# Reordering scatters, gathers and transposes in a chunk-select attention and top-1 expert kernel

## The chip, the cores and the metric

The kernel runs on one core of a Trainium2 chip. The metric is the device time of one launch in microseconds, the median of several runs. The core has four compute engines that run their own instruction streams and meet at semaphores: TensorE (PE in the profile, its weight loads PEld), VectorE (DVE), ScalarE (ACT) and GpSimd (POOL). SyncE (SP) only issues transfers. In this kernel SyncE issues the loads of q, k and v and all transposes done by DMA; GpSimd issues the weight loads and every indirect transfer (scatter and gather of token rows, scatter of the output).

## The reference

The computation has two halves. The first is attention for 4 batches, 8 heads, 768 positions and 64 elements per head, in which each query attends to six chunks of 32 keys, chosen by an upper bound made from each chunk's smallest and largest key:

```python
ub = np.sum(np.maximum(q[:, :, :, None, :] * k_min[:, :, None, :, :],
                       q[:, :, :, None, :] * k_max[:, :, None, :, :]), axis=-1)
ub = np.where(causal, ub, -1000000000.0)
top_chunks = np.argsort(ub, axis=-1)[..., -top_k:]
scores = scale * np.matmul(q, k.transpose(0, 1, 3, 2))
# mask = chunk selected and causal; softmax over what is left
return np.matmul(attn, v)
```

The second half takes the 3072 tokens of 512 elements that come out and sends each through one of 8 experts:

```python
logits = x @ w_gate
expert_idx = np.argmax(logits, axis=1)
# gate_w: the softmax probability of the chosen expert
for e in range(E):
    xe = x[expert_idx == e]
    out[expert_idx == e] = gate_w[...] * (np.maximum(xe @ w1[e], 0.0) @ w2[e])
```

## The kernel before

Two heads of a batch are one pair; there are 16 pairs, four to a batch, and one pass of the main loop for each. In pass `i` the kernel computes scores and outputs of pair `i`, prepares keys and queries of pairs `i+1` and `i+2`, and works off the router's part of pair `i-1`. The order on TensorE and GpSimd is the order in which the code is written (`manual_schedule`); in the pass loop that holds for VectorE too. ScalarE and SyncE are ordered by the scheduler, SyncE by hand in the expert part.

The steps of preparing a query (`pn` is pair `i+1`, `pj` pair `i+2`):

```python
def q_t(hf):                                   # TensorE: transpose half a query into PSUM
    pt = ps_m.tile([128, 384], FP32, tag="m")  # ps_m: 3 buffers, shared by all small results
    ...
def q_v(hf): nc.vector.tensor_copy(out=qT[:], in_=s[f"qp{hf}"][:])
def q_r(hf): nc.gpsimd.tensor_scalar(qA[:], s[f"qT{hf}"][:], 0.0, None, ALU.max)
def q_c(hf): nc.gpsimd.tensor_copy(out=qsb[0:64, 0, ts(hf, 384)], in_=s[f"qT{hf}"][0:64, :])   # cast
def q_s(hf): nc.scalar.activation(qsb[0:64, 1, ts(hf, 384)], s[f"qp{hf}"][64:128, :], AF.Copy)
def mask():                                    # TensorE: transpose the selection, 6 matmuls (L379)
    pt = ps_m.tile([64, S], BF16, tag="m")
    ...
```

Scores, outputs and denominators. `Pr` and `Pa` hold exponentials, `po` the output of one query half in PSUM (one buffer), and `ud` multiplies the summed exponentials with a column of ones, and the output with the router's weights:

```python
def scores(i, u):   # matmuls into ps (L407), Exp on ScalarE (L412), causal select on GpSimd (L416)
def av(i, u):       # po += v x P (L429)
def out_t(i, qb):   # VectorE: ot <- po (L435), frees po
def add(i, u):      # VectorE: Pa += P (L441), 128 x 768 float32
def ud():           # TensorE: pu <- Pa, ot, Pr (L464), needs all adds of the pair
```

The main loop of before, cut to what the change touches:

```python
av(i - 1, 6); out_t(i - 1, 1); load(i + 1, "v")
scores(i, 0); scores(i, 1)
r["ud"]()
if pn: pn["q_v"](1); pn["q_r"](1)
...
    route[b - 1]["rank_v"](); route[b - 1]["gate"]()       # third pair of a batch
weights(4 * i); scatters(i, 0); early(i, 0)
if i == NP - 2: table(True)
keys(j, lambda: scores(i, 2))                              # key transposes of pair i+2
av(i, 0); scores(i, 3); av(i, 1); add(i, 1); out_t(i, 0)
if pn: pn["ub"]()
...
if pn: pn["q_c"](0); pn["q_c"](1)
weights(4 * i + 1); scatters(i, 1); early(i, 1)
r["lgp_t"](); r["x_t"](0)
if pn: pn["select_t"]()
r["lgp"](); r["xr"](0)
if pn: pn["select"]()
scores(i, 4); av(i, 2)
weights(4 * i + 2); scatters(i, 2)
scores(i, 5); av(i, 3); scores(i, 6)
early(i, 2)
r["x_t"](1)
if pj: pj["q_t"](0); pj["q_t"](1); load(i + 3, "q")
r["xr"](1)
early(i, 3)
if pn: pn["mask"]()
av(i, 4)
if pj: pj["q_v"](0); pj["q_r"](0); pj["q_s"](0); pj["q_s"](1)
add(i, 3); add(i, 4); add(i, 5)
av(i, 5)
if hp == 1 and b > 0: route[b - 1]["rank"]()               # 12 small matmuls (L553 to L559)
weights(4 * i + 3); scatters(i, 3); early(i, 4)
```

Routing. When the four pairs of a batch are done, `logits`, `gate`, `rank` and `rank_v` give every token a row in `xs_dram`, sorted by expert, and `scatter(us)` writes the rows of one batch there, in six scatters of 128 tokens. `table(first)` is about 20 small VectorE instructions that work out which expert and which rows each tile of 128 tokens has. It runs twice: `table(True)` for the first NA = 11 tiles, which hold tokens of the first three batches only, and `table(False)` for the others, when the last batch is ranked.

A tile of the expert part:

```python
def gather(j):      # GpSimd: 128 rows of xs_dram -> xg_bufs[j % XB]   (XB = 8)
def x_in(j):        # SyncE: transpose by DMA, xT <- xg; then, from j = 4, tok(j)
def tok(j):         # VectorE: token numbers of the tile (L702, L704), for the output scatter
def up(j):          # TensorE: ph <- w1, xT (L715, 8 matmuls); ScalarE: h_ = relu; SyncE: hT <- h_ (L721)
def down(j):        # TensorE: py <- w2, hT (L731, 8 matmuls); ScalarE: y = gate * py (L737);
                    # GpSimd: scatter y into out (L738)
```

```python
dve.__exit__(None, None, None)            # from here on the scheduler orders VectorE
av(NP - 1, 6); out_t(NP - 1, 1)
late = list(range(6))
for n in range(4): tok(n)
with tc.manual_schedule(engines={SP, POOL}):
    up(0); rt["ud"](); up(1); x_in(4); rt["lgp_t"](); rt["x_t"](0); rt["x_t"](1); rt["lgp"]()
    r["logits"](); r["gate"](); rt["xr"](0); rt["xr"](1)
    up(2); x_in(5); down(0)
    r["rank"](); r["rank_v"](); table(False)
    # then for each tile j from 3:
        if j + 5 < hi:
            if late: r["scatter"](late[:2]); del late[:2]
            gather(j + 5)
        if j < hi: up(j)
        if j + 3 < hi: x_in(j + 3)
        if j - 2 >= lo: down(j - 2)
```

The gathers 0 to 7 are issued in the last pass of the pair loop, by `early`. 28 tiles are computed; three more are computed only if a count in the table asks for it.

## Time and profile before

The median of three runs is 362.26 us (361.37 to 362.64). The profiled execution took 368.39 us, its span from the first to the last instruction is 366.6 us.

| part of the span | from, us | to, us |
|---|---|---|
| start, pair 0 | 0 | 29.0 |
| passes 0 to 14, from one mask transpose to the next | 29.0 | 232.2 |
| last pass, up to the first expert tile | 232.2 | 247.4 |
| expert tiles 0 to 27 and the end | 247.4 | 366.6 |

How to read what follows: busy time is the union of an engine's instructions; a table of stretches gives it for any window. The timeline lists instructions in order of time, with the idle time of their engine ahead of them in square brackets and the instruction or transfer that ended it. L and a number is the line of the kernel. A wait for several semaphores is put down to the one that came last by the profile.

### The profile page before, as it was taken

How to read it: one execution, taken by the hardware profiler on the slowest of the kernel's cores; microseconds unless marked ns; L12 is line 12 of the kernel's file. 1: busy time of each engine (PE TensorE's matmuls, PEld its weight loads, DVE VectorE, ACT ScalarE, POOL GpSimd, SP SyncE). 2: the span in 40 equal slices, each digit the busy share in tenths (PEclk: the TensorE clock that was granted, in tenths of full speed). 3: DMA queues.
4: the chain of work that ended last, by engine and by line, in shares of the span. 5: the costliest groups of instructions: out<-in, count | busy, mean ns of one | idle time of the engine just before them, and what ended most of it. 6: DMA issues, size and time to landing. Idle time of an engine off the chain costs nothing.

```text
span 366.6 us, 8002 instructions
## 1 busy us (share of the span) xinstructions
PE 336.7 (92%) x2599; PEld 188.4 (51%) x2599; DVE 223.4 (61%) x748; ACT 225.6 (62%) x369; POOL 223.8 (61%) x333
## 2 busy tenths in 40 slices
PE   7779999999999999999999997979969799999980
PEld 3345666666656656565566663544423344444430
DVE  8778988979999889989788999645600000000000
ACT  3578777887787677778777864642342355445530
POOL 7437656566369994359985737774556655555331
PEclk9999999999999999999999999899999999999996
DMA  9988997999269999837999932146969999999850
GB/s 180 182 166 153 231 228 159 189 228 187 46 136 168 220 217 185 144 88 153 206 198 155 188 56 83 45 102 118 176 161 203 222 199 206 214 188 212 168 142 28
DMA packets 138184, 59.85 MB, mean 163 GB/s; under 512 B 122779, under 2 KB 130973, under 8 KB 138144
## 3 DMA queue, kind: packets, MB, share of 16 engines
q1 hardware_dynamic: 120608, 29.91, 42.0%
q0 software_dynamic: 17536, 29.42, 41.1%
q8 instruction: 23, 0.38, 0.4%
q14 instruction: 17, 0.14, 0.1%
HBM read 56.14 MB, written 10.51 MB: 182 GB/s over the span
## 4 chain that ended last, share of the span: by engine, by line
PE 46%; issue 16%; DVE 13%; POOL 13%; ACT 4%; DMA 2%; SPq 2%; POOLq 1%; DVEq 0%; ACTq 0%
PE po L429 14%; PE ps L407 8%; PE pu L464 6%; DVE Pa L441 4%; PE pu L350 4%; POOL out_dram L738 4%; PE ph L715 3%; PE pt L226 3%; PE xp L505 2%; PE py L731 2%; PE pt L244 2%; POOL xs_dram L579 2%; POOL KTE L680 2%; POOL xg L680 1%; DMA QSB<-spare 1%
## 5 line engine op out<-in xcount | busy, mean ns | idle before, releaser
L412 ACT ACTIVATE Pr<-ps 128x768 f32<-128x768 f32 (+2 forms) x112 | 66.8, 627 | 28.0 <-PE ps L407 26.1
L441 DVE TENSOR_TENSOR Pa<-Pa,Pr 128x768 f32<-128x768 f32 (+2 forms) x80 | 68.0, 850 | 7.6 <-PE po L429 2.3
L429 PE MATMUL po<-Pr,v 128*64 128x384 f32 (+2 forms) x448 | 63.8, 401 | 2.1 <-POOL Pr L416 2.1
L731 PE MATMUL py<-w_all,hT 128*128 x224 | 52.9, 379 | 3.4 <-DMA hT<-h__4156 1.3
L407 PE MATMUL ps<-QSB,KTE 128*64 128x384 bf16 (+2 forms) x576 | 55.0, 295 | 0.3 <-ACT QSB L326 0.2
L416 POOL TENSOR_SCALAR_AFFINE_SELECT Pr<-Pr 128x256 f32<-128x256 f32 x80 | 36.1, 475 | 21.8 <-ACT Pr L412 21.0
L407 PEld LDWEIGHTS <-KTE 128*64 128x64 bf16 x576 | 31.4, 110 | 26.9 <-issue 22.5
L429 PEld LDWEIGHTS po<-Pr,v 128*64 128x64 f32 x448 | 33.8, 137 | 17.8 <-POOL Pr L416 5.9
L253 POOL TENSOR_SCALAR qA<-qT 128x384 f32<-128x384 f32 x28 | 41.3, 1476 | 2.0 <-DVE qT L249 1.3
L731 PEld LDWEIGHTS <-hT 128*128 128x128 bf16 x224 | 21.9, 98 | 30.4 <-DMA hT<-h__4156 1.7
L238 ACT ACTIVATE KTE<-pt 64x384 bf16<-64x384 f32 x64 | 30.9, 482 | 4.8 <-PE pt L226 3.2
L412 ACT ACTIVATE Pa<-ps 128x768 f32<-128x768 f32 x32 | 25.9, 811 | 8.4 <-PE ps L407 7.0
L715 PE MATMUL ph<-w_all,KTE 128*128 x120 | 28.4, 379 | 2.5 <-ACT h__4156 L719 1.5
L429 PE MATMUL po<-Pa,v 128*64 128x384 f32 x128 | 26.8, 499 | 2.3 <-DVE ot L435 2.3
L738 POOL DMA_INDIRECT out_dram<-y,ti x14 | 13.9, 990 | 21.7 <-ACT y L737 19.9
L715 PE MATMUL ph<-w_all,QSB 128*128 x104 | 24.6, 379 | 1.5 <-issue 1.4
L579 POOL DMA_INDIRECT xs_dram<-xrow,sli x21 | 22.1, 1054 | 6.0 <-issue 5.5
L195 POOL DMA_DIRECT2D w_all<-in_moe_w_dram x32 | 25.3, 790 | 0.0
L234 DVE TENSOR_REDUCE kmx<-pt 128x12 f32<-128x384 f32 x32 | 17.8, 556 | 12.1 <-PE pt L226 8.5
L464 PE MATMUL pu<-Pa,dcol 128*32 128x384 f32 x128 | 20.6, 498 | 0.3 <-DVE Pa L441 0.2
L256 POOL CAST QSB<-qT 64x384 bf16<-64x384 f32 x32 | 17.2, 563 | 6.0 <-DVE qT L249 3.0
L715 PEld LDWEIGHTS <-KTE 128*128 128x128 bf16 x120 | 11.6, 97 | 17.4 <-issue 4.8
(210 smaller groups left out, 584.6 us busy)
## 6 DMA issues: line engine op xcount, KB each, us to landing
w_all<-in_moe_w_dram POOLq DMA_DIRECT2D x32, 512.0 KB
q<-in_q_dram SPq DMA_DIRECT2D x32, 192.0 KB
v<-in_v_dram SPq DMA_DIRECT2D x32, 192.0 KB
k<-in_k_dram SPq DMA_DIRECT2D x16, 192.0 KB
w_all<-in_k_dram SPq DMA_DIRECT2D x16, 192.0 KB
xs_dram<-xrow,sli POOLq DMA_INDIRECT x21
out_dram<-y,ti POOLq DMA_INDIRECT x14
xg<-xs_dram,grow POOLq DMA_INDIRECT x12
```

The costliest lines, as they stand in the source:

```text
L238: nc.scalar.activation(kte[0:64, hd, ts(hf, 384)], s[f"kp{hf}"][64 * hd:64 * hd + 64, :], AF.Copy, bias=0.0, scale=0.125)
L253: nc.gpsimd.tensor_scalar(qA[:], s[f"qT{hf}"][:], 0.0, None, ALU.max)
L407: nc.tensor.matmul(pv[c:c + CW, hd, :], lhsT=kte[:, hd, ds(kb * 128 + c, CW)], rhs=qsb[:, hd, ds(qb * 384 + 384 - w, w)], start=True, stop ...
L412: nc.scalar.activation(P[:, :, ds(c0, w)], pv, AF.Exp)
L416: nc.gpsimd.affine_select(out=pd, in_=pd, pattern=[[0, 2], [1, 128]], compare_op=ALU.is_ge, fill=0.0, base=0, channel_multiplier=-1)
L429: nc.tensor.matmul(s["po"][64 * hd:64 * hd + 64, 384 - w:384], lhsT=vt[:, kb, hd, :], rhs=P[:, hd, ds(c0, w)], start=first, stop=last and ...
L441: nc.vector.tensor_tensor(acc[:, :, 384 - w:384], acc[:, :, 384 - w:384], P[:, :, ds(c0, w)], ALU.add)
L464: nc.tensor.matmul(pu[32 * g:32 * g + 32, 384 - w:384], lhsT=lhsT, rhs=rhs, skip_group_check=True, **kw)
L579: d = nc.gpsimd.indirect_dma_start(out=xs_dram[:], out_offset=bass.IndirectOffsetOnAxis(ap=sli[:, u:u + 1], axis=0), in_=bst[b][f"xrow{u % ...
L715: nc.tensor.matmul(ph[:, fh, :], lhsT=xT[:, c, :], rhs=w_all[:, ds(wo + (c * F + fh * 512), 512)], start=(c == 0), stop=(c == NDC - 1), sk ...
L731: nc.tensor.matmul(py[:], lhsT=hT[:, c, :], rhs=w_all[:, ds(wo + (W1W + c * DM), DM)], start=(c == 0), stop=(c == NFC - 1))
L738: d = nc.gpsimd.indirect_dma_start(out=out[:], out_offset=bass.IndirectOffsetOnAxis(ap=ti[:], axis=0), in_=y, in_offset=None, bounds_check ...
```

## The change

The change moves instructions and adds buffers (three for gathered tiles, one for queries); the arithmetic stays. It is for taking GpSimd's casts, scatters and gathers and VectorE's table out of the way of steps that TensorE waits for, and for spreading the transfers of the expert part. Its parts:

- the second half of the query transposes and its copies go behind the mask transposes; the ud matmuls go behind the key transposes; one add goes ahead of the mask
- the casts of the query on GpSimd go ahead of scatters and weight issues of the pass, and one scatter of each batch moves behind the last score group of its pass
- the first table goes behind the chunk selection
- odd pairs' queries are loaded into a part of the weight buffer that is filled late, so that query loads have two buffers; three weight blocks instead of two are loaded at the start, and the block that shares that buffer late
- all eleven gathers of the first tiles are issued ahead of the expert tiles, into eleven buffers, in other places of the last pass
- the last batch's scatters go out one per tile, from tile 3 on, the first ahead of it, instead of two
- later gathers start at tile 8, and their transposes are issued two tiles ahead instead of three
- VectorE keeps its written order in the expert part too, with the token copies in fixed places

```diff
-    EARLY = 2
+    EARLY = 3
...
-        if nm == "k" and i % 2:
-            at = (E - 1) * WE + W1W + 4 * DM
+        if nm in "kq" and i % 2:
+            at = (E - 1) * WE + (W1W + 4 * DM if nm == "k" else 2 * F)
...
-    XB = 8
+    XB = NA
     def gather(j):
-        if 4 <= j < 8:
+        if 8 <= j < NA:
+            if j == 8:
+                more_x = work.tile([128, 3, XW], BF16, tag="xrow00", name="more_x")
+                xg_bufs.extend(more_x[:, n] for n in range(3))
+        elif 4 <= j < 8:
...
     def early(i, slot):
         if i == NP - 1:
-            for n in ((0, 1), (2, 3), (4, 5), (6, 7), ())[slot]:
+            for n in ((0, 1), (), (2, 3, 4), (5, 6, 7), ())[slot]:
                 gather(n)
...
             scores(i, 1)
-            r["ud"]()
+            if hp == 2 and b > 0:
+                route[b - 1]["rank_v"]()
             if pn:
                 pn["q_v"](1)
+                pn["q_s"](1)
                 pn["q_r"](1)
+                pn["q_c"](0)
+                pn["q_c"](1)
...
             weights(4 * i)
             scatters(i, 0)
             early(i, 0)
-            if i == NP - 2:
-                table(True)
-            keys(j, lambda: scores(i, 2))
+
+            def mid():
+                r["ud"]()
+                scores(i, 2)
+
+            keys(j, mid)
...
             if pn:
                 pn["select"]()
+            if i == NP - 2:
+                table(True)
...
             r["x_t"](1)
             if pj:
                 pj["q_t"](0)
-                pj["q_t"](1)
-                load(i + 3, "q")
             r["xr"](1)
+            add(i, 3)
             early(i, 3)
             if pn:
                 pn["mask"]()
+            if pj:
+                pj["q_t"](1)
+                load(i + 4, "q")
             av(i, 4)
...
         with tc.manual_schedule(engines={SP, POOL}):
+            for n in range(8, NA):
+                gather(n)
             up(0)
...
             rt["x_t"](1)
+            tok(0)
+            tok(1)
             rt["lgp"]()
...
             r["rank_v"]()
+            r["scatter"]((0,))
+            tok(4)
+            tok(5)
             table(False)
...
-                    if lo == 0 and j + 5 < hi:
-                        if late:
-                            r["scatter"](late[:2])
-                            del late[:2]
-                        gather(j + 5)
+                    if lo == 0 and j < 8:
+                        r["scatter"]((j - 2,))
+                    if lo == 0 and 8 <= j < hi - 3:
+                        gather(j + 3)
                     if j < hi:
                         up(j)
-                    if lo == 0 and j + 3 < hi:
-                        x_in(j + 3)
+                    if lo == 0 and j + 3 < NA or lo == 0 and j >= NA - 2 and j + 2 < hi:
+                        n = j + (3 if j + 3 < NA else 2)
+                        x_in(n)
+                        tok(n)
                     if j - 2 >= lo:
                         down(j - 2)
             tiles(0, JM)
+        dve.__exit__(None, None, None)
```

## The prediction

> **What bounds the kernel now.** I read the page's busy totals first, then a table of stretches cut at events of the kernel, and last the timeline inside the stretches that come out long.

> ```profile
> PE 336.7 (92%) x2599; PEld 188.4 (51%) x2599; DVE 223.4 (61%) x748; ACT 225.6 (62%) x369; POOL 223.8 (61%) x333
> ```

> TensorE at 92% says that it is the bound, not what can be won. For that I cut the span at the mask transposes (L379), which come once in each pass of the pair loop, and in the expert part at the first matmul of a tile. Columns: span, busy time (and count) of each engine, granted clock, DMA share, GB/s.

> ```profile
> 72.19:86.17 13.98, 13.98 (x132) 9.05 (x132) 11.73 (x37) 11.00 (x19) 8.90 (x17) 1.00 1.10 204
> 100.14:114.81 14.67, 14.16 (x144) 8.80 (x144) 13.65 (x48) 11.07 (x19) 11.31 (x17) 1.00 0.75 137
> 128.98:143.55 14.57, 14.48 (x131) 8.50 (x131) 12.32 (x37) 11.01 (x19) 10.06 (x18) 1.00 1.16 218
> 171.98:187.13 15.15, 13.88 (x131) 8.18 (x131) 12.63 (x37) 11.49 (x20) 13.93 (x20) 1.00 1.02 195
> 215.21:232.22 17.01, 14.25 (x131) 7.84 (x130) 14.59 (x58) 8.58 (x14) 10.72 (x16) 0.90 0.19 56
> 265.07:293.01 27.94, 22.34 (x97) 9.32 (x96) 1.28 (x9) 9.60 (x12) 17.36 (x18) 1.00 0.90 198
> 293.01:349.00 55.99, 55.68 (x257) 25.01 (x256) 2.30 (x14) 28.28 (x33) 28.28 (x28) 1.00 0.95 200
> ```

> The reader is to see a floor and what stands above it. Six of the thirteen stretches between mask transposes last 13.97 or 13.98 us with TensorE busy throughout: there it is packed, and no reordering can shorten them. The other seven are 14.67, 14.17, 14.57, 14.45, 15.15, 14.10 and 17.01. In the expert part a tile needs 16 matmuls of 0.216 us (1.73 us from one group's start to the next), 3.45 us; 265.07 to 293.01 holds six tiles, 27.94 instead of 20.7, and 293.01 to 349.00 holds sixteen at 3.50. So some 6 us in the pair loop and 7 us in the expert tiles are waits. The timeline names most of them (start, length, what ran, idle before it and its releaser):

> ```profile
> 172.47 2.57 POOL L416 TENSOR_SCALAR_AFFINE_SELECT Pr<-Pr 128x256 f32<-128x256 f32 x3
> 228.11 1.55 PE L429 MATMUL po<-Pa,v 128*64 128x384 f32 x4 [2.32 <-DVE ot L435]
> 245.35 1.52 PE L429 MATMUL po<-Pr,v 128*64 128x384 f32 x12 [1.34 <-POOL Pr L416]
> 270.39 1.92 PE L715 MATMUL ph<-w_all,KTE 128*128 x8 [1.47 <-ACT h__4156 L719]
> 273.60 1.89 PE L731 MATMUL py<-w_all,hT 128*128 x8 [1.29 <-DMA hT<-h__4156]
> ```

> At 172 us the causal selects on GpSimd start only after 8 us of casts, scatters and weight issues in a row (164.86 to 172.47). At 228 TensorE waits for the copy that empties po, because VectorE has just worked off the first table, 221.26 to 226.38. At 245 four gathers stood ahead of the selects (238.93 to 244.26). From 262 on it is transfers: ScalarE's wait for h__4156, 6.8 us, is the longest there, and the trace doesn't say convincingly what released it.

> [...] two selects took 1.48 us at 232.57 and a scatter 1.51 at 234.22 beside VectorE's adds, against 0.77 and 0.97 to 1.1 elsewhere. [...] from 300 to 345 us the two queues take 65.1% and 32.9%. [...] the last hT transpose shows 1.23 us from 352.02, and TensorE uses its data at 355.30.

> **The change part by part.** No arithmetic goes away: the count of matmuls, activations and transfers stays. Everything is order, and three buffers.

> *Pair loop.* (a) The denominator matmuls (ud) move behind the key transposes, the add of unit 3 ahead of the mask. In 128.98 to 143.55 the chain of waits runs through three adds of 1.10, 1.34 and 1.08 us that end at 133.10, and ud starts at 133.15; with 0.8 us of key transposes ahead of it and one add earlier, that 0.6 us is hidden. (b) The query's second transposes go behind the mask transposes, so that the mask need not find its PSUM bank as a fourth beside three others (bufs=3); the trace shows 0.7 us of waits for it in all. (c) The casts go ahead of scatters and weight issues. That takes nothing off GpSimd (13.93 of 15.15 us busy in the worst stretch), but the casts are now out of the way before the selects matter. Of the six long stretches before the last, the surplus over 13.98 is 0.69+0.19+0.59+0.47+1.17+0.12 = 3.2 us; 0.45 us in two of them is the rank matmuls, real work. Of the 2.3 us left I take three quarters: **-1.8**.

> (d) The first table moves behind the selection, when po has been emptied. The 2.32 us wait at 228 goes. But its 5 us of VectorE work now stands before three adds, 3.1 us, in a pass where VectorE works 14.59 us, so a part may come back as a wait for the accumulators: **-2.0**.

> *Entry to the expert part.* (e) Two gathers instead of four ahead of the selects, and VectorE kept in program order, so that the token copies (L702, waiting for gathers at 242.25, 243.49, 244.99, 246.33) no longer hold up the adds: TensorE can start the first tile 1.4 us earlier and its later 0.25 us wait goes, about -1.8. (f) Against it: nine gathers now come in a row on GpSimd. One takes 1.0 us and the next starts 0.30 later, so 9 x 1.32 = 11.9 us, from 244.3 to 256.2, and behind them stands the addition of the last logits (0.65 us), which ran at 255.09. From its end to the one-hot took 1.5 us: 256.9 + 1.5 = 258.4, against the rank matmuls at 257.87 now. The gain of (e) is thus lost again at the rank matmuls: **0**.

> *Tiles.* (g) Before, tiles 3 to 5 each issue two scatters, a gather and an output scatter: four at 1.3 us, 5.2 us of GpSimd in a 3.45 us tile, and the transfers on top of transposes. After, tiles 3 to 7 have one scatter and one output, 2.6 us, and gathers 8 to 10 fall into a stretch with the DMA engines some 60% busy (244 to 256). If this overload is the cause, most of the 7.2 us goes; since h__4156's wait isn't explained, I take a little over half: **-4.0**. (h) From tile 11 on the input transpose is issued two tiles ahead, not three, and it stands behind the hidden transpose on SyncE. In the steady part tile 24 starts at 338.64, its hT transpose at 341.66 (3.02 later), the input transpose behind it at 342.99 (4.35 later). The packets of both, about 1,600, counted microsecond by microsecond, end some 6.7 us after that tile's start and 6.4 us after tile 22's; with the 0.3 us or so between the last tile's hT packets (about 355.0) and their use at 355.30, data are ready at 6.7 to 7.0. Needed: 2 x 3.453 = 6.91. That is a tie. At 0.05 us a tile for 16 tiles: **+0.8**.

> (i) A third early weight and a second query buffer: the first 44 us wait for VectorE (13.61 of 15.24 us busy in 29.00 to 44.24), so nothing: **0**.

> Sum: -1.8 - 2.0 + 0 - 4.0 + 0.8 = **-7.0 us**; 362.26 - 7.0 = **355.3 us**.

> **The rivals.** *The input transpose becomes the bound* (h). With the wait for both transposes at 8 us instead of 6.9, a tile takes 4.0 us, since the loop closes over two tiles: (4.35 + 3.65)/2. Sixteen tiles cost 9 us and the time is about 362 to 364. For it: the DMA engines are 99% busy from 300 to 345. Against it: the packet counts. *The gather chain starves the tiles:* gathers from 11 on now start at tile 8, only one tile ahead of their transpose. Gather 11 starts some 2.4 us into tile 8 and lands about 3.3 us after its start (238.93 to 242.25 in the first one), 5.7; its transpose is issued at 3.45 + 4.35 = 7.8. It holds with 2 us to spare. *Nothing of the tile part is won,* because the 7.2 us come from something else than the order of GpSimd's transfers, or belong to the profiled execution only (its device time was 368.39 us against 362.26): then (g) is 0 and the time is 359. *Everything is won:* (d), (g) and (a) to (c) in full give -3 -7 -2.3 +0.8, about 351.

> **Range and chances.** The middle case is 355.3. The full gain, 351, sets the low end at 350.5; the tie in (h) turning out badly while the rest holds, 355.3 + 5, sets the high end at 360.5. Faster by 2% means under 355.0, so the middle lies on the line: 0.45. Slower by 2% needs 369.5, more than the worst rival: 0.05. Within 2%: 0.50.

> **What will show it.** (a) to (c): the six stretches near 14.0, with 14.4 where rank lies. (d): no wait of po for ot L435 in pass 14. (e), (f): the first tile starts earlier against the mask before it, and a wait of 1 to 2 us ahead of pr L553 on VectorE's one-hot. (g): tiles 5 to 11 at about 3.6 us each. (h): no waits, or short ones, of PEld L715 (its new line) for KTE and QSB transposes from tile 11 on; tiles at 3.5. The prediction is wrong if that last number is 3.7 or more, or if tiles 5 to 11 stay at 4.6.

## The result, and the profile after

The changed kernel takes 394.67 us (median of four executions, 393.15 to 395.22) against 362.45 us for the kernel before (361.37 to 362.67) on the same chip: ratio 1.0889, 95% interval 1.0851 to 1.0927. It is slower by 32 us where 7 us of gain were predicted.

First the page's engine totals of the changed kernel:

```profile
PE 337.8 (86%) x2599; PEld 182.1 (47%) x2599; DVE 221.3 (57%) x748; ACT 226.2 (58%) x369; POOL 230.0 (59%) x333
```

TensorE is busy 337.8 us against 336.7, and the span is 391.0 against 366.6 us: all but about a microsecond of the difference is time in which TensorE waits. Where it waits, the table of stretches of the changed kernel shows, cut at the same events (span, busy time and count of PE, PEld, DVE, ACT, POOL, then granted clock, DMA share, GB/s). The first line is one plain pass of the pair loop, the second pass 14, then from the last mask to tile 0, tiles 0 to 5, 5 to 11, and 11 to 27:

```profile
59.80:74.61 14.81, 13.77 (x131) 8.34 (x131) 11.55 (x37) 10.97 (x20) 9.01 (x14) 1.00 1.01 181
227.33:240.43 13.10, 13.10 (x134) 7.65 (x134) 11.55 (x42) 8.81 (x15) 10.64 (x13) 1.00 0.28 47
240.43:261.66 21.23, 15.91 (x125) 7.95 (x124) 12.85 (x32) 8.44 (x14) 13.19 (x20) 0.84 0.32 79
261.66:283.30 21.64, 18.60 (x106) 8.48 (x106) 10.67 (x57) 7.00 (x9) 13.93 (x16) 0.92 0.76 163
283.30:306.12 22.82, 20.88 (x98) 9.40 (x96) 0.99 (x8) 10.95 (x13) 12.80 (x13) 1.00 1.06 219
306.12:373.47 67.35, 57.14 (x257) 24.94 (x257) 2.38 (x15) 26.67 (x31) 29.49 (x30) 1.00 0.74 164
```

| stretch | before, us | after, us | difference |
|---|---|---|---|
| start to the last mask | 232.22 | 240.43 | +8.2 |
| last mask to tile 0 | 15.15 | 21.23 | +6.1 |
| tiles 0 to 5 | 17.70 | 21.64 | +3.9 |
| tiles 5 to 11 | 27.94 | 22.82 | -5.1 |
| tiles 11 to 27 | 55.99 | 67.35 | +11.4 |
| tile 27 to the end | 17.6 | 17.5 | -0.1 |

The sum is +24.4 us, the difference of the two spans. It is less than the 32 us between the medians because the profiled execution of the kernel before was six microseconds longer than its median, and that of the changed kernel 1.5 us shorter.

The waits stand in the timeline of TensorE in the changed kernel (start, length, what ran, and in brackets the idle time before it and what ended it):

```profile
65.40 0.85 PE L464 MATMUL pu<-Pa,dcol 128*32 128x384 f32 x8 [1.04 <-ACT QSB L266]
249.07 0.86 PE L464 MATMUL pu<-Pa,dcol 128*32 128x384 f32 x3 [4.24 <-DVE Pa L441]
274.45 0.22 PE L553 MATMUL pr<-oh,U 128*128 128x48 bf16 x1 [2.06 <-DVE oh L530]
323.60 1.89 PE L717 MATMUL ph<-w_all,QSB 128*128 x8 [2.42 <-DMA QSB<-xg]
332.44 1.89 PE L717 MATMUL ph<-w_all,QSB 128*128 x8 [1.77 <-DMA QSB<-xg]
```

There are four kinds, one for each loss. **At 65.40** the denominator matmuls (ud) wait for ScalarE's copy q_s(1) (L266). ud reads nothing that this copy writes; the two have only a PSUM pool in common. The page's group table of the changed kernel shows that this is the rule (busy, mean ns | idle before, releaser):

```profile
L464 PE MATMUL pu<-Pa,dcol 128*32 128x384 f32 x128 | 15.8, 536 | 17.7 <-ACT QSB L266 13.5
```

13.5 us of idle time stand ahead of ud for this copy alone. **At 249.07** ud waits for the additions, which stand behind the table on VectorE. VectorE's timeline, from the table's last operation on:

```profile
245.36 0.17 DVE L646 SCALAR_TENSOR_TENSOR grow<-ej,loc 128x11 int32<-128x11 f32 x1
245.44 0.55 DVE L509 TENSOR_TENSOR xrow<-xp,rec 128x384 bf16<-128x384 f32 x1
245.91 3.10 DVE L441 TENSOR_TENSOR Pa<-Pa,Pr 128x768 f32<-128x768 f32 x3
```

**At 274.45** the rank matmuls wait for the one-hot. It is made from the last logits, and their addition on GpSimd runs only at 272.52, behind nine gathers in a row (260.53 to 272.50). **From tile 11 on** the tiles wait for their input transposes.

### The profile page after: what moved, and what is told of

Same layout as the page of the kernel before. It is cut to its first block, busy times and chain, and to the rows that moved or that the text cites. A ratio compares the mean times of both kernels' runs of the same rounds, so it can differ in the third digit from the quotient of the medians.

```text
span 391.0 us, 8009 instructions
## 1 busy us (share of the span) xinstructions
PE 337.8 (86%) x2599; PEld 182.1 (47%) x2599; DVE 221.3 (57%) x748; ACT 226.2 (58%) x369; POOL 230.0 (59%) x333
## 4 chain that ended last, share of the span: by engine, by line
PE 45%; issue 18%; DVE 12%; POOL 10%; ACT 6%; DMA 6%; POOLq 1%; DVEq 0%; ACTq 0%
PE po L429 15%; PE ps L407 9%; PE pu L464 6%; PE pu L350 6%; DVE Pa L441 5%; ACT Pr L412 3%; POOL out_dram L740 3%; PE xp L505 2%; PE pt L244 2%; POOL xg L684 2%; PE lgp L483 2%; ACT QSB L266 2%; POOL xs_dram L579 2%; PE selp L358 2%; DMA more_x<-xs_dram,grow 2%
## 5 line engine op out<-in xcount | busy, mean ns | idle before, releaser
L412 ACT ACTIVATE Pr<-ps 128x768 f32<-128x768 f32 (+2 forms) x112 | 66.8, 628 | 27.0 <-PE ps L407 24.2
L441 DVE TENSOR_TENSOR Pa<-Pa,Pr 128x768 f32<-128x768 f32 (+2 forms) x80 | 65.9, 823 | 19.6 <-PE po L429 14.1
L429 PE MATMUL po<-Pr,v 128*64 128x384 f32 (+2 forms) x448 | 62.0, 399 | 0.3 <-POOL Pr L416 0.3
L416 POOL TENSOR_SCALAR_AFFINE_SELECT Pr<-Pr 128x256 f32<-128x256 f32 x80 | 43.6, 568 | 30.1 <-ACT Pr L412 29.5
L253 POOL TENSOR_SCALAR qA<-qT 128x384 f32<-128x384 f32 x28 | 38.7, 1383 | 3.8 <-DVE qT L249 3.7
L429 PEld LDWEIGHTS po<-Pr,v 128*64 128x64 f32 x448 | 30.1, 137 | 20.4 <-issue 11.7
L412 ACT ACTIVATE Pa<-ps 128x768 f32<-128x768 f32 x32 | 25.9, 808 | 14.4 <-PE ps L407 14.4
L717 PE MATMUL ph<-w_all,KTE 128*128 x120 | 28.3, 379 | 5.6 <-DMA KTE<-xg 1.7
L717 PE MATMUL ph<-w_all,QSB 128*128 x104 | 26.0, 394 | 7.4 <-DMA QSB<-xg 4.2
L464 PE MATMUL pu<-Pa,dcol 128*32 128x384 f32 x128 | 15.8, 536 | 17.7 <-ACT QSB L266 13.5
L579 POOL DMA_INDIRECT xs_dram<-xrow,sli x21 | 24.3, 1159 | 5.6 <-issue 4.7
L429 PE MATMUL po<-Pa,v 128*64 128x384 f32 x128 | 26.7, 498 | 0.0
L740 POOL DMA_INDIRECT out_dram<-y,ti x14 | 13.8, 988 | 21.1 <-ACT y L739 21.1
L195 POOL DMA_DIRECT2D w_all<-in_moe_w_dram x32 | 25.6, 801 | 0.0
L234 DVE TENSOR_REDUCE kmx<-pt 128x12 f32<-128x384 f32 x32 | 17.6, 548 | 8.4 <-ACT KTE L238 8.2
L499 POOL TENSOR_TENSOR lg<-lg,lgt 128x48 f32<-128x48 f32 x24 | 6.9, 289 | 24.4 <-DVE lgt L490 23.4
L509 DVE TENSOR_TENSOR xrow<-xp,rec 128x384 bf16<-128x384 f32 x28 | 15.4, 552 | 10.4 <-PE xp L505 10.3
```

Of the source, the lines that this page charges most:

```text
L195: d = nc.gpsimd.dma_start(out=dst, in_=src.rearrange("(c p) f -> p c f", p=128))
L412: nc.scalar.activation(P[:, :, ds(c0, w)], pv, AF.Exp)
L416: nc.gpsimd.affine_select(out=pd, in_=pd, pattern=[[0, 2], [1, 128]], compare_op=ALU.is_ge, fill=0.0, base=0, channel_multiplier=-1)
L429: nc.tensor.matmul(s["po"][64 * hd:64 * hd + 64, 384 - w:384], lhsT=vt[:, kb, hd, :], rhs=P[:, hd, ds(c0, w)], start=first, stop=last and ...
L441: nc.vector.tensor_tensor(acc[:, :, 384 - w:384], acc[:, :, 384 - w:384], P[:, :, ds(c0, w)], ALU.add)
L464: nc.tensor.matmul(pu[32 * g:32 * g + 32, 384 - w:384], lhsT=lhsT, rhs=rhs, skip_group_check=True, **kw)
```

## The experiments

*How to read them.* The runs of one batch share a chip, and the ratio is always to the kernel before on that chip. Chips differ: the kernel before has a median of 362 to 363 us on some (as above) and of 369 to 370 us on others. The microseconds of different batches are therefore not to be subtracted; the stretches of the traces can be compared, with care for tiles 5 to 11, which vary most. "Passes" is a plain pass of the pair loop. All stretches are from mask and tile starts in the trace of each run.

| run | kernel before, us | ratio (95%) | passes | last mask at | to tile 0 | 0 to 5 | 5 to 11 | 11 to 27 |
|---|---|---|---|---|---|---|---|---|
| before | 362 | 1 | 13.98 | 232.2 | 15.2 | 17.7 | 27.9 | 56.0 |
| after | 362 | 1.089 (1.085 to 1.093) | 14.81 | 240.4 | 21.2 | 21.6 | 22.8 | 67.4 |
| c0_before_again | 370 | - | 13.97 | 232.2 | 14.8 | 18.3 | 28.3 | 55.6 |
| e9_before_once_more | 370 | - | 13.97 | 231.7 | 15.5 | 18.1 | 28.9 | 56.4 |
| a0_after_again | 369 | 1.072 (1.065 to 1.078) | 14.81 | 238.9 | 19.7 | 21.7 | 25.6 | 67.8 |
| e1_ud_ahead | 370 | 1.028 (1.022 to 1.034) | 13.85 | 225.6 | 19.9 | 20.4 | 26.1 | 64.5 |
| e4_copies_same_pass | 369 | one execution | 13.70 | 225.0 | 20.2 | 20.6 | 25.4 | 66.0 |
| e2_three_ahead | 370 | 1.037 (1.032 to 1.042) | 14.81 | 240.6 | 21.1 | 21.7 | 23.1 | 58.7 |
| e12_ud_and_three_ahead | 369 | 1.000 (0.997 to 1.002) | 13.86 | 225.7 | 21.5 | 24.6 | 23.1 | 57.1 |
| e3_table_behind_adds | 370 | 1.069 (1.061 to 1.077) | 14.81 | 240.5 | 19.3 | 24.0 | 24.9 | 70.7 |
| e5_gathers_behind_logits | 369 | one execution | 14.81 | 240.4 | 21.0 | 18.6 | 27.3 | 69.1 |
| e11_after_with_old_entry | 370 | 1.066 (1.060 to 1.073) | 14.81 | 241.8 | 17.8 | 17.1 | 27.9 | 69.7 |
| e7_old_table_and_gather_places | 363 | 1.001 (0.998 to 1.003) | 13.70 | 228.8 | 17.8 | 17.4 | 24.2 | 56.9 |
| e8_table_in_five_pieces | 363 | 0.996 (0.993 to 1.000) | 13.70 | 224.7 | 19.6 | 16.6 | 24.2 | 56.9 |
| e6_pair_loop_only | 363 | 0.992 (0.990 to 0.995) | 13.70 | 227.4 | 15.8 | 17.8 | 22.9 | 55.3 |
| e13_pair_loop_only_again | 363 | 0.994 (0.991 to 0.996) | 13.70 | 228.4 | 16.1 | 18.1 | 22.9 | 56.1 |
| e10_pair_loop_and_table_pieces | 370 | 0.996 (0.994 to 0.999) | 13.70 | 224.6 | 21.2 | 17.4 | 28.0 | 58.9 |
| e14_pieces_and_program_order | 362 | 0.993 (0.990 to 0.995) | 13.70 | 224.7 | 18.4 | 17.0 | 23.1 | 55.3 |
| e15_pair_loop_and_program_order | 362 | 0.996 (0.994 to 0.999) | 13.70 | 227.5 | 17.5 | 17.4 | 22.7 | 56.4 |

### The pair loop: a ring of three buffers

ps_m is a pool of three PSUM buffers that go round in program order. In the changed kernel the order near the pass boundary is q_t(0), mask, q_t(1), then in the next pass the two key transposes, and ud. ud is the third behind q_t(1), so it gets q_t(1)'s buffer, and that is free only when the copies q_v(1) and q_s(1) have read it. They stand in the next pass: q_v(1) did so in the kernel before, too; q_s(1) was put there by the change, and on ScalarE it comes behind exponentials. Theory A: this ring is the cost. The rival: the exponentials are simply late, and the wait would move to the next score matmuls. ScalarE's timeline in the changed kernel shows what stood ahead of the copy:

```profile
63.26 0.81 ACT L412 ACTIVATE Pa<-ps 128x768 f32<-128x768 f32 x1 [0.76 <-PE ps L407]
63.97 0.87 ACT L412 ACTIVATE Pr<-ps 128x512 f32<-128x512 f32 x2
64.86 0.49 ACT L266 ACTIVATE QSB<-pt 64x384 bf16<-64x384 f32 x1
```

The copy ends at 65.35, and ud starts at 65.40. Two edits of the changed kernel open the ring in different ways. The first puts ud back ahead of the key transposes, so that another tile than ud inherits the buffer:

```
     scores(i, 1)
+    r["ud"]()
...
     def mid():
-        r["ud"]()
         scores(i, 2)
```

> The changed kernel with only the ud matmuls back ahead of the key transposes. Theory A (PSUM ring): ud takes the third PSUM buffer behind the two key transposes, which is the one that holds the query's second half until ScalarE copies it (L266) behind the exponentials; with ud first, the ring has a free buffer, the 1.04 us wait of ud goes, a plain pass takes 13.98 us instead of 14.81 and the time falls by 10 to 12 us, to about 383. Theory B (the passes are longer because of the casts and adds that moved on GpSimd and VectorE): a pass stays near 14.8 and the time moves by less than 3 us.

The second leaves ud where the change put it and empties the buffer in the pass that filled it:

```
     if pj:                      # behind mask and q_t(1)
         pj["q_v"](0)
         pj["q_r"](0)
         pj["q_s"](0)
+        pj["q_v"](1)
+        pj["q_s"](1)
...
     if pn:                      # next pass
-        pn["q_v"](1)
-        pn["q_s"](1)
```

> The changed kernel with ud left behind the key transposes, but the second half's copies (VectorE's qT and ScalarE's QSB, which empty its PSUM buffer) in the pass of its transposes instead of the next. Theory A (ud waits for that buffer): the buffer is empty before ud comes, the 1.04 us wait goes and a plain pass takes 13.9 to 14.1 us, the time falls by 10 us or more. Theory B (it is ud's place behind the keys, or the order on ScalarE after it, that costs): a pass stays above 14.5.

Both took the wait away: a plain pass took 13.85 and 13.70 us, the last mask came at 225.6 and 225.0 us instead of 240.4. Theory A holds, and more was won than expected, for the ring had also hidden what the new order is worth. The stretch of a plain pass with the copies in their own pass:

```profile
58.00:71.70 13.70, 13.70 (x134) 8.34 (x132) 11.91 (x37) 10.73 (x20) 8.39 (x15) 1.00 1.05 192
```

Compare this with the 13.98 us of the kernel before, busy throughout as well. TensorE counted as busy all the time, and yet there were 0.28 us to win; its weight loads fell from 9.05 to 8.34 us. Why the same work packs better in this order was not tested.

The same pair loop in the kernel before, with table, gathers, scatters and tiles as they were there (the edit is the change's pair loop with the four lines above, its third early weight and its second query buffer):

> The kernel before with the pair loop of the run that emptied the second query transpose's buffer in its own pass, and nothing else of the change: table, early gathers, scatters of the last batch and the expert tiles stand as in the kernel before. Theory A (the order of the pair loop was worth having, and cost only because the ring of three buffers closed): passes of about 13.70 us against 13.97, the last mask some 6 to 7 us earlier than in the kernel before, stretches behind it as before (15, 18, 28, 56 us), ratio about 0.98. Theory B (what the pair loop gains is given back where the GpSimd queue or the weights set the pace): passes as in A, but the stretches behind the last mask longer by as much, ratio 0.995 to 1.00.

> The run with the pair loop alone, once more, timed in more rounds. Theory A (the stall in tiles 5 to 11 belongs to the execution's transfers, not to the order of the pair loop): where the kernel before takes about 370 us, tiles 5 to 11 take 26 to 29 us here too, the passes stay at 13.70 us, and the ratio is 0.985 to 0.995; where it takes 362 to 363, they take about 23 us again and the ratio repeats 0.992. Theory B (the new order of the pair loop also removes the stall): where the kernel before takes 370 us, tiles 5 to 11 take 23 us and the ratio is 0.97 to 0.98.

Ratios 0.992 and 0.994, the two of them on different chips. This part of the change alone is an improvement, small (under 1%) but clear of the noise, of 2.5 to 3.7 us. In the first run Theory A held for the passes, and the stretches behind the last mask stayed as before or fell; but the last mask came 4.8 us earlier and not 6 to 7, and the ratio of 0.98 was not reached. A part of the ring is left: in the passes with rank, 14.93 and 14.92 us against 14.67 and 14.45 in the kernel before, ud waits 0.62 us for VectorE. By the order of the code it inherits the buffer of the ranks there; this was read from the code and not tested. The second run met a chip where the kernel before takes 363 us, so it repeats the result and doesn't tell its theories apart.

### Tiles from 11 on: two or three ahead

Theory A: an input transpose two tiles ahead arrives late, every time. The rival: tile 11 and its followers are late because gathers are. The edit puts the transpose three tiles ahead again, and the gather four:

```
-    if lo == 0 and 8 <= j < hi - 3:
-        gather(j + 3)
+    if lo == 0 and 7 <= j < hi - 4:
+        gather(j + 4)
...
-    n = j + (3 if j + 3 < NA else 2)
+    n = j + 3
```

> The changed kernel with the input transposes of the late tiles three tiles ahead again (as before the change) and their gathers four ahead, from tile 7. Theory A (the loop of two tiles closes over the input transpose, 4.35 us after a tile's start plus more than 3 us of flight): tiles 11 to 27 return from 4.2 to about 3.5 us each, 10 to 12 us less, about 383. Theory B (the gathers start too late behind the one-per-tile scatters): tiles 11 and 12 still wait for their gathers and a good part of the loss stays, gain below 5 us.

Tiles 11 to 27 took 58.68 us instead of 67.35. The stretch of that run:

```profile
306.45:365.13 58.68, 55.79 (x257) 25.01 (x256) 2.45 (x15) 28.07 (x33) 30.39 (x30) 1.00 0.91 198
```

How long the transposes are under way, the timeline of SyncE's queue in the changed kernel shows (start and length of the issue, here 1.19 to 1.25 us, which is not the movement: the first issue for QSB ends at 319.59, and TensorE uses its data at 323.60). The two of QSB feed the tiles that start at 323.60 and 332.44 above, the one of hT ahead of each is the hidden transpose of an earlier tile:

```profile
317.02 1.23 SPq L723 DMA_TRANSPOSE hT<-h__4465  x1
318.34 1.25 SPq L696 DMA_TRANSPOSE QSB<-xg  x1
326.62 1.23 SPq L723 DMA_TRANSPOSE hT<-h__4536  x1
328.29 1.19 SPq L696 DMA_TRANSPOSE QSB<-xg  x1
```

From issue to use 5.26 and 4.15 us. Over tiles 11 to 27 it was 3.46 to 5.27 us, 4.1 in the mean, and the issue came 4.30 to 5.02 us after the start of the tile two before, 4.45 in the mean, where the prediction had 4.35. The time from issue to use is what was too long: two tiles of 3.45 us, less those 4.35 us, leave 2.6 us for it. The stretch of the changed kernel gives 67.35/16 = 4.21 us a tile.

The edit moves gather and transpose together, so it doesn't separate the two. The trace of the changed kernel does: from tile 12 on every gather has landed at least 2.0 us before its transpose is issued, and most transposes go out right behind the hidden transpose, as in the lines above. Only tile 11's transpose (301.81) waited for its gather, which landed at 301.80. The rival thus holds for tile 11 alone.

The two repairs together:

> The changed kernel with both: ud ahead of the key transposes, and input transposes three tiles ahead with gathers four ahead. If the two costs are independent, as theory A has it (one lies in the pair loop, one in the late tiles), the gains add: 17 us from the first (391.0 to 373.9 in the profiled spans) and 8 to 9 from the second, a span of 365 to 367 and a ratio to before of 0.99 to 1.005. If the tiles run slower because they come earlier or fuller against the transfers (theory B), less than 5 us of the second is seen and the ratio stays above 1.01.

They add up: ratio 1.000 (0.997 to 1.002), where the changed kernel had 1.072 on that chip. What keeps it from being faster than the kernel before is the entry, 21.5 and 24.6 us (this profile is of an execution of 371.3 us, against a median of 369.7, but e1 and e2 have a long entry too: 19.9 and 20.4, 21.1 and 21.7 us).

### The entry: table, gathers, and a clock that falls

Three edits of the changed kernel were tried here, and none made it faster by more than the noise. First, the table behind xr(1) and the additions:

```
     if pn:
         pn["select"]()
-    if i == NP - 2:
-        table(True)
...
     add(i, 5)                   # the pass's last addition
+    if i == NP - 2:
+        table(True)
```

> The changed kernel with the first table moved once more, behind the three adds of its pass. Theory A (the table's 5.6 us on VectorE hold up the adds, for which ud waits 4.24 us in the last pass): that wait goes and the time falls by 4 to 6 us, to about 389. Theory B (VectorE is simply full in that stretch, the first gathers wait for the table instead and give the time back at the first tiles): gain below 2 us.

Next, gathers 8 to 10 behind the last logits, instead of ahead of the first tile:

```
-    for n in range(8, NA):
-        gather(n)
     up(0)
...
     rt["lgp"]()                 # the last addition of the logits
+    for n in range(8, NA):
+        gather(n)
     r["logits"]()
     r["gate"]()
```

> The changed kernel with gathers 8 to 10 behind the last addition of the logits on GpSimd instead of ahead of it. Theory A (the nine gathers in a row hold up the logits, hence the 2.06 us wait ahead of the rank matmuls, L553): that addition comes 3.9 us earlier, the wait goes, and the stretch from the first to the sixth tile's start falls from 21.6 to about 19.5 us. Theory B (VectorE or the first transposes set that stretch): it stays within 0.7 us of 21.6.

Last, the whole entry as it was before: table ahead of the key transposes, gathers two at a place, and gathers 8 to 10 with the last scatters:

> The changed kernel with only the entry put back: table ahead of the key transposes, eight gathers at two per place in the last pass, gathers 8 to 10 with the scatters of the last batch. Pair loop (passes of 14.81 us) and late tiles (input transposes two ahead) stay as in the changed kernel. Theory A (the entry's loss of 10 us is the table's and the gathers' place): last mask at about 242 to 244 us (the table's wait of 2 to 3 us comes back ahead of it), last mask to the first tile 15 to 18 us against 21, tiles 0 to 5 about 17.5 us against 21.6, tiles 11 to 27 still 66 to 70 us; in all some 5 to 7 us less than the changed kernel. Theory B (the longer pair loop itself delays the entry, wherever table and gathers stand): last mask to tile 5 still takes 39 us or more, and the time is that of the changed kernel within 2 us.

The first turned ud's wait of 4.24 us (3.26 in a0_after_again) into one of 3.57 for the next thing that VectorE owed, and the rank matmuls waited longer, 3.98 us. Its ratio, 1.069, is the changed kernel's: Theory B. TensorE's timeline of that run:

```profile
250.15 0.51 PE L464 MATMUL pu<-ot,wgb 128*32 128x384 f32 x1 [3.57 <-DVE ot L435]
274.60 0.20 PE L553 MATMUL pr<-oh,U 128*128 128x48 bf16 x1 [3.98 <-DVE oh L530]
```

The second took 3.1 us off tiles 0 to 5 compared with a0_after_again on the same chip, as its Theory A said, and tiles 5 to 27 then took 3.0 us more. The third behaved as its Theory A said up to tile 5, which started at 276.67 us against 280.36 in a0_after_again and 283.30 in the first trace; at tile 11 only 1.3 to 1.5 us of that were left (304.60 against 305.93 and 306.12), at tile 27 nothing (374.27 against 373.75 and 373.47). The ratios, 1.066 and 1.072, can't be told apart, and Theory A's 5 to 7 us of gain did not come. One reason is in the next run, where the pair loop and the late tiles are repaired too:

> The changed kernel with the copies of the second query transpose in their own pass, the input transposes three tiles ahead with gathers four ahead, and the entry as in the kernel before: the table ahead of the key transposes, eight gathers at two per place in the last pass. Gathers 8 to 10 stand with the scatters of the last batch. Theory A (the entry's loss of about 10 us came from the table's new place and the nine gathers in a row): last mask at about 228 (the table's wait of about 2 to 3 us comes back ahead of it), last mask to the first tile 15 to 17 us against 20 to 21, tiles 0 to 5 18 to 19 us, 5 to 11 23 to 25, 11 to 27 57 to 59; ratio about 0.98. Theory B (the entry is set by the first eight gathers' transfers and the input transposes wherever the table stands, because the pair loop now ends sooner): last mask to the first tile stays at 19 us or more, ratio 0.995 to 1.005.

Its ratio of 1.001 is Theory B's, its stretch from the last mask to tile 0, 17.8 us, lies between the two. Its timelines of GpSimd, of SyncE's queue and of TensorE:

```profile
275.02 0.97 POOL L579 DMA_INDIRECT xs_dram<-xrow,sli  x1 [0.30 <-issue]
280.73 1.05 POOL L684 DMA_INDIRECT KTE<-xs_dram,grow  x1 [4.74 <-DMA xs_dram<-xrow,sli]
```

```profile
284.06 1.19 SPq L696 DMA_TRANSPOSE QSB<-KTE  x1
```

```profile
288.18 2.66 PE L717 MATMUL ph<-w_all,QSB 128*128 x8 [3.03 <-issue]
```

Gather 11 reads rows of the last batch, so it waits until the last scatter has landed. One scatter per tile puts that last scatter at 275.02, at tile 7, and gather 11 waits 4.74 us; its transpose is issued at 284.06, and tile 11 (288.18) stands after a wait of 3.03 us, for which the trace itself names no releaser. With the old tile part, two scatters at a time, tile 11 has no such wait (e6_pair_loop_only: 1.57 us at 283.90, for ScalarE). An entry that is earlier thus only waits longer at tile 11. That this is where the gains of e5 and e11 went is argued from the traces (their gather 11 waits 0.89 and 1.08 us for the last scatter, their tile 11 2.63 and 3.00 us), and was not tested alone.

The clock is the other half of the entry. This table of stretches of the changed kernel covers the time right after the wait of 4.24 us, the 2 us behind that, and the time after the wait of 2.06 us (the clock is the third column from the right):

```profile
249.07:254.07 5.00, 5.00 (x30) 2.03 (x32) 0.42 (x2) 1.30 (x2) 2.29 (x3) 0.51 0.26 66
254.07:256.07 2.00, 2.00 (x24) 1.41 (x22) 1.86 (x5) 0.81 (x1) 0.00 (x0) 1.00 0.52 101
274.45:277.45 3.00, 2.96 (x18) 1.27 (x19) 2.77 (x19) 0.98 (x2) 1.24 (x2) 0.50 0.48 90
```

After each of the two waits TensorE runs at half its clock (0.50), until 253.97 and 277.86. The two stretches of the kernel before, last mask to tile 0 and tiles 0 to 5, to be compared with the third and fourth line of the first table above:

```profile
232.22:247.37 15.15, 13.31 (x125) 7.83 (x124) 7.71 (x17) 8.26 (x14) 12.18 (x17) 1.00 0.31 79
247.37:265.07 17.70, 17.45 (x105) 8.28 (x105) 10.74 (x52) 6.09 (x8) 8.59 (x10) 1.00 0.76 139
```

TensorE's idle time in the entry grew from 2.1 to 8.4 us, which is about the two waits (4.24 + 2.06), and its busy time by 3.75 us with the same matmuls but one. Half the clock for 4.9 and 3.4 us of work costs about 4.15 us, an estimate from these lines. Idle and busy time together make up the 10.0 us that the entry lost.

### Can the table be hidden at all?

The table's twenty operations were cut into five pieces and spread over pass 14 (two of its intermediate results got buffers of their own), once with the tiles of the change and once with the old ones:

```
+    if i == NP - 2:
+        next(part, None)        # one of five pieces, at five places of the pass
```

> As the run with the old places, but the table's twenty operations are spread over pass 14 in five pieces, at five places between the vector work of that pass. Theory A (what makes the table costly is that it stands in one block of over 5 us ahead of work that TensorE waits for): no wait of over 1.5 us on VectorE in pass 14 or at its end, last mask at 225 to 226, last mask to the first tile 15 to 17 us, the rest as in the run with the old places, ratio about 0.97. Theory B (the sum of VectorE's work in pass 14 is what delays, in one block or in five): the wait comes back, spread, and the ratio equals that of the run with the old places within 0.5%.

> The run with the pair loop alone, but the table's twenty operations are spread over pass 14 in five pieces. Theory A (the table's block is the last wait of the pair loop that can be had): pass 14 takes 13.2 us against 15.96, no wait over 1.5 us up to the first tile, which starts at 240 to 241 us against 243.2; ratio 0.98 to 0.985. Theory B (the pieces push the additions behind them, TensorE then waits about 2 us for them at the sums of the next pass, and its clock is halved for some 3 us after such a wait): the first tile starts at 242.5 to 244 us and the ratio is as for the pair loop alone, 0.99 to 0.995.

Pass 14 took 13.16 us in both, against 16.95 (e7), 15.96 (e6) and 17.00 (e13) with the table in one block, so the table's own wait is gone. Part of it came back as 1.95 and 1.72 us ahead of ud, in both cases for the additions behind the pieces. The clock of 0.50 that e10's Theory B expected came behind e8's 1.95 us (0.50 from 232.17 to 234.17 us), not behind e10's own 1.72 (1.00 from 231.04 to 236.04). e8's ratio is 0.4% below e7's, with intervals that overlap. In e10 a longer wait stood in the last pass, and the first tile started at 245.85 us, later than either theory had it; the clock was 0.50 from 241.60 to 242.60, behind that wait. TensorE's and VectorE's timelines of e10:

```profile
239.60 0.87 PE L429 MATMUL po<-Pa,v 128*64 128x384 f32 x4 [3.75 <-DVE ot L435]
```

```profile
237.25 0.15 DVE L712 COPY ti<-KTE 128x1 int32<-128x1 int32 x1 [2.78 <-DMA KTE<-xs_dram,grow]
238.57 0.15 DVE L712 COPY ti<-KTE 128x1 int32<-128x1 int32 x1 [1.17 <-DMA KTE<-xs_dram,grow]
238.66 0.43 DVE L441 TENSOR_TENSOR Pa<-Pa,Pr 128x256 f32<-128x256 f32 x1
239.00 0.55 DVE L435 COPY ot<-po 128x384 f32<-128x384 f32 x1
```

Two token copies of 0.15 us each wait for gathers, and the addition and the copy that TensorE needs stand behind them. That is the wait which the change's step (e), program order on VectorE to the end, was for. So this step was tried alone, once with the pieces and once with the table in one block at its old place:

```
-dve.__exit__(None, None, None)  # ahead of the expert part
...
     tiles(0, JM)
+dve.__exit__(None, None, None)
```

> The run with the pair loop alone and the table in five pieces, and VectorE kept in program order to the end of the expert tiles, so that the token copies stand behind the last pass's additions. Theory A (step e is right: the token copies hold up the additions, and program order takes that away): no wait of 3.75 us at the last pass, the first tile starts at 241 to 242 us against 245.9, and the ratio is 0.975 to 0.985. Theory B (the first tile is then held by its input transpose or the gathers instead): the first tile starts at 244 us or later and the ratio is 0.99 to 1.00.

> The run with the pair loop alone (table in one block at its old place), and VectorE kept in program order to the end. Theory A: the waits before the first tile grow no longer, the first tile starts at 242 to 243 us, ratio 0.985 to 0.99, and the table in pieces is worth another 1 to 2 us beside it. Theory B: program order gains nothing where the table stands at its old place, the ratio repeats 0.992 to 0.994.

The 3.75 us are gone, tile 0 starts at 243.05 instead of 245.85 us. That lies between the two theories; the ratio, 0.993, is Theory B's and no better than that of the pair loop alone. A wait of 1.95 us ahead of ud and half a clock behind it (0.50 from 233.15 to 234.15 us, 0.91 in the mean of the stretch) remain:

```profile
224.68:243.05 18.37, 15.27 (x125) 8.00 (x124) 11.86 (x27) 8.32 (x14) 15.04 (x22) 0.91 0.49 116
```

That stretch took 15.8 us in e6_pair_loop_only at full clock. With the table in one block the ratio was 0.996 and its Theory B nearly right: the causal selects then kept TensorE waiting 2.34 us at 242.43. Program order thus removed the wait for token copies that e10 showed, and brought no ratio below the 0.992 of the pair loop alone.

### What the kernel before does in tiles 5 to 11

The changed kernel took 5.1 us less there than the kernel before. Is that a gain of the change? The kernel before and the changed one were run again for it:

> The kernel before, unchanged, profiled once more. Theory A: the 27.94 us that six expert tiles took from 265.07 to 293.01 belong to that one execution, since it took 368.39 us of device time against 362.26 in the timed runs; a second profile then shows the six tiles from the sixth tile's first matmul at 21 to 23 us and a span near 361. Theory B: they belong to the kernel (two scatters, a gather and an output a tile overload GpSimd and the transfers); they are again 26 to 29 us.

> The changed kernel, unchanged, timed once more beside the kernel before on the chip of these runs, as a base for the others. Expected: the ratio on record within 1%, 1.08 to 1.10, if chips differ only by a common factor; nearer to 1.07 (391.0 to 366.6, the ratio of the two profiled spans) if a part of the 8.9% was a difference between chips.

> The kernel before, unchanged, for one more profile. Both profiles of it so far are of executions of 368.4 and 368.6 us, while many of its executions take 362. Theory A (the stall of about 7 us in tiles 5 to 11 is what separates 368 from 362): if this execution takes about 362 us, tiles 5 to 11 take 21 to 23 us and the rest is as before; if it takes 368 or more, they take about 28 us again. Theory B (the two levels differ elsewhere, in the pair loop or at the end): at 362 us tiles 5 to 11 take 28 us all the same.

The ratio of a0, 1.072, is its second case: part of the 8.9% was a difference between chips. The changed kernel takes 397.0 us on this one against 394.7, the kernel before 369.5 against 362.5.

In the kernel before the 28 us came again both times, 28.3 and 28.9; in the changed one, on its other chip, the stretch took 25.6. But all three profiled executions of the kernel before are long ones: 368.4, 368.6 and 369.9 us. The last two met a chip on which every execution of it takes 366 us or more; one of 362 us was never caught in a profile, so e9's first condition didn't occur, and only its second one, 28 us at 368 us or more, was seen to hold. The next two lines are tiles 5 to 11 of e9 and of e13:

```profile
265.33:294.27 28.94, 22.84 (x97) 9.43 (x96) 1.48 (x10) 10.52 (x13) 17.34 (x18) 0.98 0.88 198
```

```profile
262.52:285.44 22.92, 21.12 (x97) 9.39 (x96) 1.29 (x9) 10.95 (x13) 16.22 (x17) 1.00 1.08 215
```

e13 has the tile part of the kernel before unchanged, two scatters and a gather per tile and all, and needs 22.9 us. Two groups of chips have to be kept apart here. Where the kernel before takes 369 to 370 us, the runs with gathers 8 to 10 ahead of the expert tiles need 23.1 to 26.1 us for tiles 5 to 11 (a0, e1, e2, e3, e4, e12), and those without need 27.3 to 28.9 (c0, e5, e9, e10, e11), e11 with the spread scatters among them. There the early gathers seem to relieve the stall, not the spread scatters; as the entry differs between these runs too, this is a pattern and not a test. Where the kernel before takes 362 to 363 us, e6, e13, e14 and e15 need 22.7 to 23.1 us with the old gathers, and nothing of the 5 us is left to win (e7 and e8, with the spread scatters, need 24.2). What makes the stall, and whether the executions of 362 us have it, stays open.

## Why the prediction was wrong

**(a) to (c), pair loop, -1.8 predicted, +8.2 measured together with the first half of (d).** The step that failed is (a) with (b): moving ud behind the key transposes and q_t(1) behind the mask. I looked at what each moved piece waits for by its data, and in (b) even at the three buffers, but for the mask only. I didn't go round the ring once more: ud came to inherit q_t(1)'s buffer, whose last readers stand in the next pass, one of them (q_s(1)) put there by the change itself. It cost 0.83 us in a plain pass and more in the two with rank: 16.34 us against 14.67, and 17.92 against 14.45, where two waits close together (0.75 and 1.08 us, at 170.50 and 172.11) also halved the clock for 3.4 us. And it covered up an order that is good. "There it is packed, and no reordering can shorten them" was wrong too: 13.98 became 13.70. My own table showed that busy time is no measure of headroom here (14.25 us busy with 131 matmuls in pass 14, 13.98 with 132 in a plain pass), and still I used a fully busy stretch as a floor.

**(d), the table, -2.0.** Its first half came, and larger: pass 14 fell from 17.01 to 13.10 us, more than the wait of 2.32 us, because half a clock had followed that wait in the kernel before (0.50 from 227.85 to 231.26). Its second half, "a part may come back as a wait for the accumulators", was right in kind and too small: 4.24 us instead of some part of 2.3, and behind it half a clock, about 2.45 us (half of 4.9). Between the select and ud stand 5.6 us of table (239.81 to 245.44), xr(1) and 3.1 us of additions; ud needs the last of them. That sum could have been made beforehand.

**(e) and (f), entry, 0.** (f)'s mechanism came as described, a wait at the rank matmuls of 2.06 us. (e) was right about the token copies (e10 shows their wait, e14 shows it gone), but in the changed kernel nothing of it was left to see. What the two together missed is that the nine gathers would start at 260.53 instead of 244.3 us, because everything ahead of them was late, and again the clock (0.50 up to 253.97, and from 274.44 to 277.86). That the nine take 11.9 us was right (11.97).

**(g), tiles 5 to 11, -4.0.** The trace shows -5.1, and where the kernel before takes 370 us the early gathers go with a shorter stretch. But the old tile part does it in 22.9 us as well where it takes 362 (e6, e13), which speaks for the rival "nothing of the tile part is won", that those microseconds belong to the profiled execution only. The price of the spread scatters had no place in the working: gather 11 waits for the last of them.

**(h), input transposes, +0.8 predicted, +11.4 measured.** Here the mechanism was right, and named as a rival with its formula and with 4.0 us a tile. The term that was mis-sized is the flight: I counted packets and put the data at 2.35 to 2.65 us after the issue of the transpose; the tiles could use them after 3.46 to 5.27, 4.1 in the mean. The sign named for being wrong, 3.7 us a tile or more, came with 4.21. Counting when packets move did not tell here when a consumer may start. (The two queues whose shares the prediction gives for 300 to 345 us are SyncE's, with 65.1% of the time of the 16 DMA engines, and GpSimd's, with 32.9%.) "It is a tie" should have made me distrust a sum of two estimates, and the range ended at 360.5, below the rival's own 362 to 364.

**(i), 0:** the last mask of e6 came 4.8 us earlier, the passes gave it; the start gave nothing that the trace shows (first mask at 29.0 us in both).

## What to carry to other kernels

When an instruction is moved in a program with a rotating pool, write down the ring for the new order, for every tile that lies on it: who inherits whose buffer, and where the last reader of that buffer stands. Keep the last reader close behind its producer: with the copies in their own pass, a plain pass fell from 14.81 to 13.70 us (e4). When a step comes out as a tie, take the distance that leaves room: a late tile took 4.21 us with its transpose two tiles ahead, and 3.67 with three (e2). And a wait removed at the entry of a later stage is only worth what that stage's own last arrival leaves of it: e11 was 3.7 us ahead of a0_after_again at tile 5, 1.3 at tile 11, and not ahead at tile 27.

## What the runs showed of the hardware

| idle time in the step, us | steps | next step at half clock |
|---|---|---|
| under 1.75 | all the others | 0 |
| 1.75 to 2.03 | 18 | 10 |
| over 2.03 | 23 | 23 |

In these traces it is not the length of a single wait that goes with the half clock (of the 23 waits of 1.9 to 2.5 us, 11 were followed by the half clock), but how much idle time falls into one step. The ends of matmuls in a trace are modelled, so the band in the middle may be the error of reading. Three pairs of steps show it, of the kernel before, of e9 (the same kernel) and of the changed kernel; idle time is the length less the first busy time, and the clock is the third column from the right:

```profile
224.44:227.85 3.41, 1.35 (x12) 0.69 (x10) 3.03 (x14) 1.11 (x2) 2.21 (x3) 1.00 0.19 68
227.85:231.26 3.41, 3.15 (x12) 1.32 (x14) 3.02 (x19) 0.81 (x1) 1.56 (x3) 0.50 0.08 25
```

```profile
224.80:228.21 3.41, 1.70 (x15) 1.04 (x13) 3.00 (x15) 1.30 (x2) 2.50 (x4) 1.00 0.22 78
228.21:231.62 3.41, 2.65 (x23) 1.48 (x23) 3.34 (x20) 1.42 (x3) 1.82 (x4) 1.00 0.13 44
```

```profile
168.63:172.04 3.41, 1.64 (x18) 1.05 (x14) 3.24 (x15) 2.53 (x6) 2.11 (x5) 1.00 0.75 171
172.04:175.45 3.41, 3.34 (x24) 1.38 (x26) 1.55 (x4) 1.82 (x5) 3.10 (x6) 0.50 0.76 125
```

The same wait stood in both executions of the kernel before, of 2.32 and 2.26 us. In the first 2.06 us of it fell into one step, and the next ran at half clock; in the second the end of a step cut it into 1.71 us and the rest, and the clock stayed. A wait of 3.57 us in e3 stayed without effect in the same way, cut into 1.74 and 1.84 us. In the changed kernel two short waits, 0.75 and 1.08 us, fell into one step and brought the clock down. A step that ran at half clock itself was followed by another one with less idle time: with 0.90 to 1.93 us in all five cases, with 0.67 or less in none of 33.

A wait of 2 us in this kernel can so cost about 3.7 us, an estimate from these stretches: its own length and half of 3.41.
